# Longer VectorE times in the planner, output banks handed on one by one, and 320 bytes in front of the left side of SBUF

## The chip, the cores and the metric

The kernel runs on one core of a Trainium2 chip. The metric is the device time of one execution in microseconds (us), as a median of several runs. The engines are named as in the profile: PE multiplies matrices (PEld is its loading of weights), DVE is VectorE, ACT is ScalarE, POOL is GpSimd, and SP issues the DMAs. PSUM has eight banks, named here by their tags: ab0 to ab2, at0, at1, m0 to m2.

## The reference

Three stages follow each other, all in float32. First a linear attention with decay over 4 batches, 8 heads, 768 steps and a head width of 48; then two gated products with weights of their own.

```
state = zeros(B, H, D, D)
for t in range(S):
    y[t] = r[t] . (state + (u*k[t]) v[t]^T);  state = w*state + k[t] v[t]^T
x = y laid out as 3072 tokens x 384
x = ((x @ w_a) * (x @ w_b)) @ w_out                  # 1536 wide
a, b = x @ w1, x @ w2                                 # 1024 wide
out = (((a * b) @ w3) @ w_out2)
```

The inputs arrive as 64-bit floats for the weights, which the kernel converts itself.

## The kernel before, in words

**Numbers.** Every large product is made from float32 operands that are split into a high and a low part (a cast on ACT makes the high part, a subtraction on DVE the low one), and three matmuls high*high, high*low, low*high stand for one product.

**Stages.** From 0 to some 190 us the order is written by hand: the first attention units, the conversion of the first weights, the first gated product. All behind it is a list of 2225 tasks that `plan()` (from L209) puts in order at build time. In order of time these are: the attention units that are left with the first gated product beside them (`block1`, L904; matmuls L755 into banks ab, and L808 to L810 into m0 to m2); the conversion of the later weights and the sums over them (lines 1062 to 1178); the folding of w3 and w_out2 into one matrix `wf` (L1258); and three passes over two token blocks each, called pairs here (the loop at L1316).

**A pair.** w1 and w2 are applied by a scheme with fewer multiplications: 15 combinations S of the input blocks (POOL adds them, L1332; ACT and DVE split them, L1341 and L1343) are multiplied with combinations of the weights (`prod`, L1350, 45 matmuls of 512 columns per group of columns; the moving operand is S, in tiles qw2 to qw5 or qxa, qxb; the weights are in tiles tg). DVE and ACT add the products up in SBUF (L1417, L1423), and DVE or POOL multiplies the two halves (`finish_col`, L1361). Each of the 8 blocks that this gives for each of the two column halves n is split (gh on ACT at L1443, gl on DVE at L1445) and multiplied with `wf` (L1453 to L1455, 12 matmuls of 384 columns, three for each of four token tiles b, added up over the 8 blocks in four PSUM banks). The four banks are then copied out (ACT at L1473 for even b, DVE at L1471 for odd b) into one of the output buffers, and SP stores them (L1478).

**What sets the order.** `plan()` keeps for each engine the time from which it is free. Of all tasks whose inputs are done it starts the one that can begin first, and among those of one engine that can begin within 0.01 us, the one of lowest `prio`. A task begins when its engine is free, its inputs have ended (plus `LAT`, 0.15, when they come from another engine), and a buffer of its pool is free; `plan()` picks the buffer too. It then runs the task's function, which emits the instructions. So the durations given to the tasks set nothing but the order of the instructions on each engine, and the choice of buffers. On the chip each engine works its instructions off in that order, each as soon as its semaphores allow. The durations stand at L864: D_TT for a DVE operation on 512 columns, D_A for an ACT one, D_P for POOL, MM for a matmul.

```
            at = max(at, d.end + (0 if d.eng == e else LAT))
            x = min((x for x in c if x[0] <= t0 + 0.01), key=lambda x: x[1])
        t.end = at + t.dur
        D_TT, D_A, D_P, MM = 0.70, 0.60, 1.45, 0.2275
```

**Output banks.** The four banks of one output (m0, m1, m2, at1) are one `Slot`, taken as a whole by the first of the 8 steps of a column half, and free when all four copies are done. For the very last half the banks are ab0, ab1, ab2 and at0. There are three output buffers (`out_s`, the three parts of tile x7).

**SBUF.** Pools const, wabp and att lie at the left side, in that order from low addresses upward; the others at the right side, from the top downward. wabp holds the weights of the first product, and later qw2 to qw5 and `wf`. All tiles of wabp begin 160 bytes past a multiple of 512. The tiles of the right side that feed PE (xt, later qxa and qxb; gh and gl; the weights tg; and w_out) begin 480 bytes past one.

Of the kernel before, what the change touches and what calls it, by code (L numbers as in the profile page):

```python
# [7 lines left out]
F32 = mybir.dt.float32  # L8
# [10 lines left out]
B, H, S, D = 4, 8, 768, 48  # L19
# [4 lines left out]
DM = H * D  # L24
# [23 lines left out]

END_0 = 4
LATE = 3  # L50
N_OK = 2 * 128 * N64 + 112 * NP


# [148 lines left out]


LAT = 0.15
DMA_0, DMA_MB = 2.0, 5.0


def plan(tasks):


    free, waits, users, ready = {}, {}, {}, []
    dma = 0.0
    for t in tasks:
        waits[t] = len(t.deps)
        for d in t.deps:
            users.setdefault(d, []).append(t)
    ready = [t for t in tasks if not t.deps]

    def start(t):
        e = t.eng  # L220
        at = free.get(e, 0.0)
        for d in t.deps:
            at = max(at, d.end + (0 if d.eng == e else LAT))
        picks = []
        for b in t.bufs:
            best = None
            for s in b.pool:
                if s in picks or any(u.end is None for u in s.users):
                    continue
                k = max([at] + [u.end + (0 if u.eng == e else LAT) for u in s.users])  # L230
                old = max([0.0] + [u.end for u in s.users])
                if best is None or (k, old) < best[:2]:
                    best = (k, old, s)
            if best is None:
                return None
            at = best[0]
            picks.append(best[2])
        return at, picks

    total = len(tasks)  # L240
    while ready:
        by = {}
        for t in ready:
            r = start(t)
            if r is not None:
                by.setdefault(t.eng, []).append((r[0], t.prio, t, r[1]))
        assert by, "no task can start"
        best = None
        for c in by.values():
            t0 = min(x[0] for x in c)  # L250
            x = min((x for x in c if x[0] <= t0 + 0.01), key=lambda x: x[1])
            if best is None or x[0] < best[0]:
                best = x
        at, _, t, picks = best
        t.start = at
        free[t.eng] = at + t.dur
        t.end = at + t.dur
        if t.size:
            dma = max(dma, t.end) + t.size * DMA_MB
            t.end = dma + DMA_0  # L260
        for b, s in zip(t.bufs, picks):
            s.users = b.users or [t]
            b.ap = b.get(s.key)
        t.fn()
        ready.remove(t)
        total -= 1
        for u in users.get(t, ()):
            waits[u] -= 1
            if not waits[u]:
                ready.append(u)  # L270
    assert not total
# [3 lines left out]
def rwkv_moe_kernel(ctx, tc, rkT, nat, wu, wab, wout, w12, w3T, wo2, r_in, k_in, v_in, w_in, u_in, out):  # L275
# [12 lines left out]

    with tc.manual_schedule():
        const = tc.alloc_tile_pool(name="const", bufs=1, side="left")  # L290
        wabp = tc.alloc_tile_pool(name="wabp", bufs=1, side="left")
        att = tc.alloc_tile_pool(name="att", bufs=2, side="left")
        xtp = tc.alloc_tile_pool(name="xtp", bufs=1, side="right")
# [567 lines left out]
                t.end = 0.0  # L861
            tasks.clear()

        D_TT, D_A, D_P, MM = 0.70, 0.60, 1.45, 0.2275  # L864
        CONV = 9000.0

        def g_get(key):
# [356 lines left out]

        R5 = 200.0 * (NB - 2)
        ab_b, m_t, md_last = t_ab, t_m, d
        o_slot = Slot(("m0", "m1", "m2", "at1"))

        w_t, wo2_t = {}, {}

# [12 lines left out]
        for i in range(NF2):  # L1243
# [31 lines left out]
            e1 = use(task("ACT", 0.45, eh, [last, ab_b[2 * (i // 4) + 1]], R5 + 12 * i + 32), bp)  # L1275
            e2 = use(task("DVE", 0.55, el, [e1], R5 + 12 * i + 32), bp)
            fold_end.append(e2)
        o_slot.users = mb.users + fold_end + units


        s_s, t_s = [], []
# [3 lines left out]
        for i in range(3):  # L1285
            t_s += [Slot(f"wo{p}{i}", [m_t[4 * i + 3]]) for p in "hl"]
        v_s = [Slot((f"x{i}", k), folds) for i in (0, 1, 2, 3, 5, 6) for k in range(KD)]
        out_s = [Slot(("x7", k), folds) for k in range(KD)]
        old = [x_b[NB - 2].users[i] for i in range(len(x_b[NB - 2].users))]
        c0_s = [Slot(("xa", k), old) for k in range(2 * KD - 1)]  # L1290
        c0_bufs = []
# [12 lines left out]
        left_l = task("SP", 0.1, load_left, folds, R5 + 150, size=0.66)  # L1304

        gord = (1, 0, 2, 3, 4, 5, 6, 7)
        o_last, o_users = None, o_slot.users
        PER = 1000.0
        for pair in range(NB // 2):
            base = PER * (pair + 2)  # L1310
# [27 lines left out]
            for d in range(len(SEQ)):  # L1338
                bs = Buf(s_s + xa_s if pair else s_s, s_get)
                f, dep, b0 = src[f"S{d}"]  # L1340
                hi = use(task("ACT", D_A, lambda f=f, bs=bs: nc.scalar.copy(out=bs.ap[0], in_=f()), [dep],  # L1341
                              base - 100 + S_RANK.index(d), [bs]), b0)
                lo = use(task("DVE", D_TT, lambda f=f, bs=bs: nc.vector.tensor_tensor(  # L1343
                    out=bs.ap[1], in0=f(), in1=bs.ap[0], op=ALU.subtract), [hi], base - 100 + S_RANK.index(d)), b0, bs)
                s_buf[d], s_lo[d] = bs, lo

# [87 lines left out]
            last_use = [t for t in tasks[begun:] if t.eng not in ("SP", "POOL")]  # L1434
            for n in range(2):
                end = pair == NB // 2 - 1 and n == 1
                bo = Buf([Slot(("ab0", "ab1", "ab2", "at0"), last_use)] if end else [o_slot],
                         lambda key: [psp.tile([128, DM], F32, tag=t, name="o") for t in key])
                for z, f in enumerate(gord):
                    x, dep, bv = g_b[f, n]  # L1440
                    bh = Buf(gg_s, gg_get)
                    p0 = base + 100 * z + 100 * n + 60
                    hi = use(task("ACT", D_A, lambda x=x, bh=bh: nc.scalar.copy(out=bh.ap[0], in_=x()),  # L1443
                                  [dep] + ([o_last] if o_last and not end else []), p0, [bh]), bv)
                    lo = use(task("DVE", D_TT, lambda x=x, bh=bh: nc.vector.tensor_tensor(  # L1445
                        out=bh.ap[1], in0=x(), in1=bh.ap[0], op=ALU.subtract), [hi], p0), bv, bh)

                    def go(bo=bo, bh=bh, f=f, z=z, tiles=range(B)):
                        wh, wl = (t[:, f % 4, :] for t in w_t[f // 4])
                        gh, gl = bh.ap  # L1450
                        for b in tiles:
                            cs = slice(b * C, (b + 1) * C)
                            mm(bo.ap[b], lhsT=gh[:, cs], rhs=wh, start=(z == 0), stop=False)  # L1453
                            mm(bo.ap[b], lhsT=gh[:, cs], rhs=wl, start=False, stop=False)  # L1454
                            mm(bo.ap[b], lhsT=gl[:, cs], rhs=wh, start=False, stop=(z == NF2 - 1))  # L1455

                    p0, deps = base + (240 + 40 * z if n == 0 else 950 + 36 * z), [lo, fold_end[f]]
                    if z < NF2 - 1:
                        ot = use(task("PE", 12 * 0.177, go, deps + ([ot] if z else []), p0, [bo] if z == 0 else []),
                                 bh, bo)  # L1460
                    else:
                        ot = [use(task("PE", 3 * 0.177, lambda go=go, b=b: go(tiles=[b]), deps + [ot], p0 + b), bh, bo)
                              for b in range(B)]
                    o_last = hi
                for b in range(B):
                    be = Buf(out_s, v_get)
                    c, bt = divmod(b, 2)

                    def ev(be=be, bo=bo, b=b):
                        if b % 2:  # L1470
                            nc.vector.tensor_copy(out=be.ap[:, 0:DM], in_=bo.ap[b])  # L1471
                        else:
                            nc.scalar.copy(out=be.ap[:, 0:DM], in_=bo.ap[b])  # L1473

                    e = use(task(("ACT", "DVE")[b % 2], 0.5, ev, [ot[b]], base + 900, [be]), bo)

                    def st_out(be=be, r0=(2 * n + bt) * S + (2 * pair + c) * C):
                        nc.sync.dma_start(out=out[r0:r0 + C, :], in_=be.ap[:, 0:DM])  # L1478

                    use(task("SP", 0.1, st_out, [e], base + 900, size=0.2), be)  # L1480


        cnt = const.tile([1, 1], I32, name="cnt")

        def count():
            ok = gp.tile([128, N64, 2], F32, tag="g1", name="ok")
            nc.vector.tensor_scalar(out=ok[:, :, 0], in0=chk[:, :, 0], scalar1=SQ_HI, scalar2=None, op0=ALU.is_le)
            nc.vector.tensor_scalar(out=ok[:, :, 1], in0=chk[:, :, 1], scalar1=511.5, scalar2=None, op0=ALU.is_ge)
            col = const.tile([128, 2], F32, name="col")
            nc.vector.tensor_reduce(out=col[:, 0:1], in_=flat(ok), op=ALU.add, axis=AX.X)  # L1490
            nc.vector.tensor_reduce(out=col[0:112, 1:2], in_=wok, op=ALU.add, axis=AX.X)
            nc.vector.tensor_tensor(out=col[0:112, 0:1], in0=col[0:112, 0:1], in1=col[0:112, 1:2], op=ALU.add)
            ones = const.tile([128, 1], F32, name="ones")
            nc.vector.memset(ones, 1.0)
            mid_t["count"] = col, ones
# [260 lines left out]
```

## Time and profile before

| | us |
|---|---|
| median of 3 runs | 906.73 |
| lowest and highest run | 901.91, 906.95 |
| the profiled execution, its own time | 908.81 |
| its span, first to last instruction | 907.0 |
| busy in the span: PE, DVE, ACT, POOL | 869.5, 601.3, 372.8, 204.0 |

The profiled execution is one of its own and not among the three runs; 1.8 us of its time lie outside its span. In the rows, a line such as L1445 is a line of the kernel; "out<-in" are tile names; an "x3" merges instructions that follow each other; square brackets give the time for which the engine had been idle before the instruction, and what ended it. PE's records overlap: a matmul of 512 columns is shown with 0.39 us, though the next one starts some 0.23 us behind it.

### The profile page before, as it was taken

The page shows a single profiled execution, that of the slowest core. Times are in us where ns is not written, and L with a number is a line of the kernel's source. Part 1 is how long each engine was busy: PE and PEld are TensorE (multiplying, and loading weights), DVE is VectorE, ACT ScalarE, POOL GpSimd, SP SyncE. Part 2 cuts the span into 40 slices and gives each one's busy share as a digit, 9 for nine tenths or more (in the row PEclk, how much of TensorE's full clock was granted, in tenths as well). Part 3 has the DMA queues.
Part 4 walks back from the last instruction along what each step waited for, and adds up shares of the span by engine and source line. Part 5 has one row for each costly group of instructions (what it writes and reads, how often), then busy time and mean ns, then how long its engine had stood idle before and what let it go on. Part 6 is the DMA issues. An engine that isn't in the chain of part 4 may idle for free.

```text
span 907.0 us, 13215 instructions
## 1 busy us (share of the span) xinstructions
PE 869.5 (96%) x4827; PEld 731.2 (81%) x4827; DVE 601.3 (66%) x1031; ACT 372.8 (41%) x865; POOL 204.0 (22%) x170
## 2 busy tenths in 40 slices
PE   8887899999999999999999999999998999999996
PEld 7665778888878888888888789888886888788886
DVE  8898876368989759753566368626569546954642
ACT  3555465434454344232246445425245232623221
POOL 2213300025444205300200302212325301511210
PEclk9698899999999999999999999999999999999998
DMA  8644432045867545722153324036544234423302
GB/s 268 195 148 151 138 117 93 24 129 187 243 214 209 184 137 190 211 83 88 41 146 116 105 73 150 22 111 202 157 152 152 92 122 142 149 93 98 112 1 73
DMA packets 55719, 120.54 MB, mean 133 GB/s; under 512 B 6176, under 2 KB 33440, under 8 KB 55648
## 3 DMA queue, kind: packets, MB, share of 16 engines
q1 hardware_dynamic: 55648, 119.63, 42.0%
q8 instruction: 40, 0.66, 0.3%
q14 instruction: 31, 0.25, 0.1%
HBM read 94.57 MB, written 23.07 MB: 130 GB/s over the span
## 4 chain that ended last, share of the span: by engine, by line
PE 83%; DVE 10%; DMA 2%; issue 2%; ACT 1%; SPq 0%; DVEq 0%; ACTq 0%
PE ab L755 31%; PE ab L1350 12%; PE m L808 5%; PE m L810 5%; PE m L809 5%; PE at L1350 4%; PE at L1258 4%; PE o L1453 3%; PE o L1455 3%; PE o L1454 3%; PE at L533 3%; PE at L493 2%; PE at L529 2%; DMA rk<-in_rkT_dram 1%; DVE qx L1423 1%
## 5 line engine op out<-in xcount | busy, mean ns | idle before, releaser
L1423 DVE TENSOR_TENSOR qx<-qx,ab 128x512 f32<-128x512 f32 x97 | 65.0, 684 | 33.4 <-PE ab L1350 32.1
L809 PE MATMUL m<-gl,woh 128*128 128x512 f32 x216 | 84.4, 391 | 1.5 <-DVE gl L919 1.5
L808 PE MATMUL m<-gh,woh 128*128 128x512 f32 x216 | 85.6, 396 | 0.0
L810 PE MATMUL m<-gh,wol 128*128 128x512 f32 x216 | 84.4, 391 | 0.8 <-DVE wol L162 0.8
L914 DVE TENSOR_TENSOR ab<-g,ab 128x512 f32<-128x512 f32 x54 | 37.5, 695 | 71.1 <-PE ab L755 63.2
L916 ACT CAST gh<-ab 128x512 fp32r<-128x512 f32 x54 | 31.7, 586 | 100.5 <-DVE ab L914 100.5
L1445 DVE TENSOR_TENSOR gl<-qx,gh 128x512 fp32r<-128x512 f32 x48 | 40.3, 844 | 45.8 <-ACT gh L1443 45.7
L1361 POOL TENSOR_TENSOR qx<-qx,qx 128x512 f32<-128x512 f32 x27 | 36.6, 1357 | 141.1 <-DVE qx L1423 108.4
L913 ACT COPY g<-ab 128x512 f32<-128x512 f32 x54 | 31.8, 588 | 83.6 <-PE ab L755 83.6
L1417 ACT ACTIVATE qx<-ab 128x512 f32<-128x512 f32 x55 | 32.6, 600 | 74.3 <-PE ab L1350 73.1
L1443 ACT CAST gh<-qx 128x512 fp32r<-128x512 f32 x48 | 29.5, 620 | 62.3 <-PE o L1454 59.6
L755 PE MATMUL ab<-xt,wab0h 128*128 128x512 f32 x144 | 48.1, 415 | 1.5 <-DVE xt L558 1.5
L809 PEld LDWEIGHTS m<-gl,woh 128*128 128x128 f32 x216 | 40.5, 188 | 9.9 <-DVE gl L919 1.9
L810 PEld LDWEIGHTS m<-gh,wol 128*128 128x128 f32 x216 | 40.5, 188 | 9.7 <-DVE wol L162 1.2
L486 POOL TENSOR_TENSOR kn<-natt,tnat 128x384 f32<-128x384 f32 x13 | 13.9, 1071 | 152.6 <-PE at L605 152.6
L808 PEld LDWEIGHTS m<-gh,woh 128*128 128x128 f32 x216 | 40.5, 188 | 9.5 <-ACT woh L142 0.3
L755 PE MATMUL ab<-xt,wab1h 128*128 128x512 f32 x144 | 47.3, 411 | 0.6 <-ACT g L913 0.6
L919 DVE TENSOR_TENSOR gl<-ab,gh 128x512 fp32r<-128x512 f32 x54 | 37.1, 687 | 14.9 <-ACT gh L916 14.6
L755 PE MATMUL ab<-xt,wab2h 128*128 128x512 f32 x144 | 45.5, 397 | 0.0
L465 POOL TENSOR_TENSOR rk<-rk,tr 112x512 f32<-112x512 f32 x16 | 20.8, 1299 | 109.4 <-DMA rk<-in_rkT_dram 109.4
L755 PE MATMUL ab<-xt,wab5h 128*128 128x512 f32 x144 | 45.1, 394 | 0.0
L755 PE MATMUL ab<-xt,wab4h 128*128 128x512 f32 x144 | 45.1, 394 | 0.0
(287 smaller groups left out, 2336.6 us busy)
## 6 DMA issues: line engine op xcount, KB each, us to landing
tg<-t_d SPq DMA_DIRECT2D x45, 640.0 KB, 3.9
natt<-in_nat_dram SPq DMA_DIRECT2D x20, 576.0 KB, 5.3
rk<-in_rkT_dram SPq DMA_DIRECT2D x24, 448.0 KB, 4.6
t_d<-part SPq DMA_DIRECT2D x75, 128.0 KB, 1.8
raw<-in_wab_dram SPq DMA_DIRECT2D x18, 512.0 KB, 4.0
raw<-in_w3T_dram SPq DMA_DIRECT2D x16, 512.0 KB, 4.0
raw<-in_w_dram SPq DMA_DIRECT2D x12, 512.0 KB, 5.7
raw<-in_wout_dram SPq DMA_DIRECT2D x9, 512.0 KB, 3.5
```

The lines of the kernel that those rows point to most:

```text
L755: mm(ps, lhsT=w[i][:, k, cs], rhs=x[:, j, k, :], start=(n == 0), stop=(n == 3 * KD - 1))
L808: mm(m_ps[q][k], lhsT=wh[:, j, cs], rhs=gh, start=first, stop=False)
L809: mm(m_ps[q][k], lhsT=wh[:, j, cs], rhs=gl, start=False, stop=False)
L810: mm(m_ps[q][k], lhsT=wl[:, j, cs], rhs=gh, start=False, stop=last)
L914: mu = use(task("DVE", D_TT, lambda x=bg, y=bb: nc.vector.tensor_tensor(out=y.ap, in0=x.ap, in1=y.ap, op=ALU.mult), [ea, b], p0 + 2), bg, bb)
L919: nc.vector.tensor_tensor(out=x.ap[1], in0=y.ap, in1=x.ap[0], op=ALU.subtract)
L1258: mm(bp.ap, lhsT=b.ap[x][:, g, :], rhs=wo2_t[g // 4][y][:, g % 4, :], start=(n == 0), stop=(n == 3 * NF2 - 1))
L1350: mm(bank, lhsT=x, rhs=y, start=(start and n == 0), stop=(stop and n == 2), skip_group_check=True)
L1361: mu = use(task(eng, D_TT if inner else D_P, lambda e=e, dst=dst, xa=xa, xb=xb: e.tensor_tensor(out=dst(), in0=xa(), in1=xb(), op=ALU.mult ...
L1417: e = use(task("ACT", D_A, lambda bv=bv, b=bank[c], s=s: nc.scalar.activation(out=bv.ap, in_=b.ap, func=ACTF.Copy, scale=float(s)), [pt], ...
L1423: e = use(task("DVE", D_TT, lambda bv=bv, b=bank[c], s=s: nc.vector.tensor_tensor(out=bv.ap, in0=bv.ap, in1=b.ap, op=ALU.add if s > 0 else ...
L1445: lo = use(task("DVE", D_TT, lambda x=x, bh=bh: nc.vector.tensor_tensor(out=bh.ap[1], in0=x(), in1=bh.ap[0], op=ALU.subtract), [hi], p0), ...
```

## The change

- `plan()` adds 0.25 instead of 0.15 where a task waits for one of PE.
- D_TT goes from 0.70 to 0.72, D_A from 0.60 to 0.61. A new duration D_S, 1.0, replaces D_TT for two subtractions: the low part of S (L1343) and gl (L1445).
- Each of the output banks becomes a `Slot` of its own. The first of the 8 steps is cut into four tasks, one for each bank, as the last one was before. The copies out and their stores get a lower `prio` by 100.
- Tile g1 becomes a fourth output buffer; the small tile `ok` of the final count moves from there to tile sq.
- A tile of 320 bytes that nobody uses is allocated first in const, so that everything of the left side moves up by 320 bytes.

```diff
+PAD = 320
...
+LAT_PE = 0.25
...
+    def late(d, e):
+        return 0.0 if d.eng == e else LAT_PE if d.eng == "PE" else LAT
...
-            at = max(at, d.end + (0 if d.eng == e else LAT))
+            at = max(at, d.end + late(d, e))
...
-                k = max([at] + [u.end + (0 if u.eng == e else LAT) for u in s.users])
+                k = max([at] + [u.end + late(u, e) for u in s.users])
...
+        const.tile([128, PAD // 4], F32, name="pad")
...
-        D_TT, D_A, D_P, MM = 0.70, 0.60, 1.45, 0.2275
+        D_TT, D_S, D_A, D_P, MM = 0.72, 1.0, 0.61, 1.45, 0.2275
...
-        o_slot = Slot(("m0", "m1", "m2", "at1"))
+        o_s = [Slot(t) for t in ("m0", "m1", "m2", "at1")]
...
-        o_slot.users = mb.users + fold_end + units
+        for slot in o_s:
+            slot.users = mb.users + fold_end + units
...
-        out_s = [Slot(("x7", k), folds) for k in range(KD)]
+        out_s = [Slot(("x7", k), folds) for k in range(KD)] + [Slot(("g1", 0), list(t_ab.values()) + md_last)]
...
-                lo = use(task("DVE", D_TT, lambda f=f, bs=bs: nc.vector.tensor_tensor(
+                lo = use(task("DVE", D_S, lambda f=f, bs=bs: nc.vector.tensor_tensor(
...
-                bo = Buf([Slot(("ab0", "ab1", "ab2", "at0"), last_use)] if end else [o_slot],
-                         lambda key: [psp.tile([128, DM], F32, tag=t, name="o") for t in key])
+                bo = [Buf([Slot(t, last_use) if end else slot], lambda key: psp.tile([128, DM], F32, tag=key, name="o"))
+                      for t, slot in zip(("ab0", "ab1", "ab2", "at0"), o_s)]
...
-                    lo = use(task("DVE", D_TT, lambda x=x, bh=bh: nc.vector.tensor_tensor(
+                    lo = use(task("DVE", D_S, lambda x=x, bh=bh: nc.vector.tensor_tensor(
...
-                    if z < NF2 - 1:
-                        ot = use(task("PE", 12 * 0.177, go, deps + ([ot] if z else []), p0, [bo] if z == 0 else []),
-                                 bh, bo)
+                    if 0 < z < NF2 - 1:
+                        ot = [use(task("PE", 12 * 0.177, go, deps + ot, p0), bh, *bo)]
                     else:
-                        ot = [use(task("PE", 3 * 0.177, lambda go=go, b=b: go(tiles=[b]), deps + [ot], p0 + b), bh, bo)
-                              for b in range(B)]
+                        ot = [use(task("PE", 3 * 0.177, lambda go=go, b=b: go(tiles=[b]), deps + (ot if z else []),
+                                       p0 + b, [] if z else [bo[b]]), bh, bo[b]) for b in range(B)]
...
-                    e = use(task(("ACT", "DVE")[b % 2], 0.5, ev, [ot[b]], base + 900, [be]), bo)
+                    e = use(task(("ACT", "DVE")[b % 2], 0.5, ev, [ot[b]], base + 800, [be]), bo[b])
...
-                    use(task("SP", 0.1, st_out, [e], base + 900, size=0.2), be)
+                    use(task("SP", 0.1, st_out, [e], base + 800, size=0.2), be)
...
-            ok = gp.tile([128, N64, 2], F32, tag="g1", name="ok")
+            ok = stg.tile([128, N64, 2], F32, tag="sq", name="ok")
```

## Rows read from the trace of the kernel before

**Rows 1.** The page: busy time of each engine, and the shares of the chain.

```profile
PE 869.5 (96%) x4827; PEld 731.2 (81%) x4827; DVE 601.3 (66%) x1031; ACT 372.8 (41%) x865; POOL 204.0 (22%) x170
...
PE 83%; DVE 10%; DMA 2%; issue 2%; ACT 1%; SPq 0%; DVEq 0%; ACTq 0%
```

**Rows 2.** Stages: length, busy us of PE, PEld, DVE, ACT, POOL; clock, DMA share, GB/s.

```profile
200.00:300.00 100.00, 99.27 (x738) 81.59 (x737) 89.59 (x157) 45.80 (x128) 45.23 (x37) 1.00 0.70 207
300.00:470.00 170.00, 170.00 (x964) 139.18 (x963) 105.98 (x242) 58.67 (x164) 31.35 (x26) 1.00 0.42 132
470.00:612.00 142.00, 140.55 (x660) 121.08 (x660) 81.24 (x122) 66.61 (x146) 20.49 (x14) 1.00 0.28 97
...
694.00:708.00 14.00, 9.96 (x39) 7.97 (x38) 13.93 (x16) 3.38 (x7) 6.84 (x5) 0.88 0.41 127
708.00:783.00 75.00, 75.00 (x366) 66.04 (x365) 42.63 (x62) 26.53 (x47) 18.65 (x15) 1.00 0.36 117
783.00:798.00 15.00, 13.81 (x62) 10.77 (x62) 14.89 (x22) 6.10 (x12) 3.93 (x3) 1.00 0.51 171
```

**Rows 3.** Stages again: the 3.3 us behind the longest gap of PE.

```profile
699.70:703.00 3.30, 3.30 (x11) 2.81 (x10) 3.23 (x6) 1.41 (x3) 0.48 (x1) 0.50 0.58 175
```

**Rows 4.** Waits of PE: us in total, times, longest.

```profile
PE o L1455 <- DVE gl L1445: 3.7, 2, 3.1
...
PE m L809 <- DVE gl L919: 1.5, 1, 1.5
```

**Rows 5.** Timeline at the longest gap: start, length, engine, line.

```profile
695.58 3.42 DVE L1445 TENSOR_TENSOR gl<-qx,gh 128x512 fp32r<-128x512 f32 x2
696.75 1.71 POOL L1332 TENSOR_TENSOR qcvt<-v,qs 128x512 f32<-128x512 f32 x1
...
699.06 0.44 PE L1455 MATMUL o<-wf1h,gl 128*128 128x384 f32 x1 [3.15 <-DVE gl L1445]
```

**Rows 6.** Single lines: durations in ns, lowest, median and highest, and when.

```profile
L1445 DVE TENSOR_TENSOR gl<-qx,gh x48: 677/692/1807, 631.7 to 892.8; 128x512 fp32r<-128x512 f32 x48
...
L1343 DVE TENSOR_TENSOR qw5l<-qs,qw5h x5: 678/1362/1789, 693.9 to 786.3; 128x512 fp32r<-128x512 f32 x5
...
L1423 DVE TENSOR_TENSOR qx<-qx,ab x97: 670/686/690, 622.3 to 869.7; 128x512 f32<-128x512 f32 x97
```

**Rows 7.** Timeline of the end: the last copies out and the last matmul.

```profile
895.42 0.56 DVE L1471 COPY qx<-o 128x384 f32<-128x384 f32 x1 [1.42 <-DMA out_dram<-qx]
...
898.35 0.34 PE L1455 MATMUL o<-wf1h,gl 128*128 128x384 f32 x1
900.09 0.48 ACT L1473 COPY qx<-o 128x384 f32<-128x384 f32 x1 [2.47 <-DMA out_dram<-qx]
900.58 0.56 DVE L1471 COPY qx<-o 128x384 f32<-128x384 f32 x1 [2.30 <-ACT qx L1473]
```

**Rows 8.** Timeline of unbroken products: qxb at the right side, qw at the left.

```profile
748.99 0.85 PE L1350 MATMUL ab<-qxb,tg 128*128 128x512 f32 x3
749.68 0.39 PE L1350 MATMUL ab<-qw5h,tg 128*128 128x512 f32 x1
...
751.78 0.85 PE L1350 MATMUL ab<-qxb,tg 128*128 128x512 f32 x3
752.47 0.34 PE L1453 MATMUL o<-wf0h,gh 128*128 128x384 f32 x1
...
753.87 0.34 PE L1455 MATMUL o<-wf0h,gl 128*128 128x384 f32 x1
```

**Rows 9.** Chain in order of time: two unbroken stretches of PE.

```profile
479.79 4.12 PE ab L755 x18
...
543.41 4.18 PE at L1258 x24
```

**Rows 10.** Timeline: w_out's product, first and last of seven such starts.

```profile
502.23 0.39 PE L808 MATMUL m<-gh,woh 128*128 128x512 f32 x1
...
506.31 0.39 PE L808 MATMUL m<-gh,woh 128*128 128x512 f32 x1
```

More of the change, by code (lines that the diff above doesn't have):

```diff
@@ L1306, in rwkv_moe_kernel @@
         gord = (1, 0, 2, 3, 4, 5, 6, 7)
-        o_last, o_users = None, o_slot.users
+        o_last = None
         PER = 1000.0
@@ L1452, in go @@
                             cs = slice(b * C, (b + 1) * C)
-                            mm(bo.ap[b], lhsT=gh[:, cs], rhs=wh, start=(z == 0), stop=False)
-                            mm(bo.ap[b], lhsT=gh[:, cs], rhs=wl, start=False, stop=False)
-                            mm(bo.ap[b], lhsT=gl[:, cs], rhs=wh, start=False, stop=(z == NF2 - 1))
+                            mm(bo[b].ap, lhsT=gh[:, cs], rhs=wh, start=(z == 0), stop=False)
+                            mm(bo[b].ap, lhsT=gh[:, cs], rhs=wl, start=False, stop=False)
+                            mm(bo[b].ap, lhsT=gl[:, cs], rhs=wh, start=False, stop=(z == NF2 - 1))
                     p0, deps = base + (240 + 40 * z if n == 0 else 950 + 36 * z), [lo, fold_end[f]]
-                    if z < NF2 - 1:
-                        ot = use(task("PE", 12 * 0.177, go, deps + ([ot] if z else []), p0, [bo] if z == 0 else []),
-                                 bh, bo)
-                    else:
-                        ot = [use(task("PE", 3 * 0.177, lambda go=go, b=b: go(tiles=[b]), deps + [ot], p0 + b), bh, bo)
-                              for b in range(B)]
+                    if 0 < z < NF2 - 1:
+                        ot = [use(task("PE", 12 * 0.177, go, deps + ot, p0), bh, *bo)]
+                    else:
+                        ot = [use(task("PE", 3 * 0.177, lambda go=go, b=b: go(tiles=[b]), deps + (ot if z else []),
+                                       p0 + b, [] if z else [bo[b]]), bh, bo[b]) for b in range(B)]
                     o_last = hi
@@ L1470, in ev @@
                         if b % 2:
-                            nc.vector.tensor_copy(out=be.ap[:, 0:DM], in_=bo.ap[b])
+                            nc.vector.tensor_copy(out=be.ap[:, 0:DM], in_=bo[b].ap)
                         else:
-                            nc.scalar.copy(out=be.ap[:, 0:DM], in_=bo.ap[b])
-                    e = use(task(("ACT", "DVE")[b % 2], 0.5, ev, [ot[b]], base + 900, [be]), bo)
+                            nc.scalar.copy(out=be.ap[:, 0:DM], in_=bo[b].ap)
+                    e = use(task(("ACT", "DVE")[b % 2], 0.5, ev, [ot[b]], base + 800, [be]), bo[b])
                     def st_out(be=be, r0=(2 * n + bt) * S + (2 * pair + c) * C):
                         nc.sync.dma_start(out=out[r0:r0 + C, :], in_=be.ap[:, 0:DM])
-                    use(task("SP", 0.1, st_out, [e], base + 900, size=0.2), be)
+                    use(task("SP", 0.1, st_out, [e], base + 800, size=0.2), be)
         cnt = const.tile([1, 1], I32, name="cnt")
         def count():
-            ok = gp.tile([128, N64, 2], F32, tag="g1", name="ok")
+            ok = stg.tile([128, N64, 2], F32, tag="sq", name="ok")
             nc.vector.tensor_scalar(out=ok[:, :, 0], in0=chk[:, :, 0], scalar1=SQ_HI, scalar2=None, op0=ALU.is_le)
```

## The prediction

> **What bounds the kernel now.** I read the page's busy times first, then a table of stages, then what PE waited for, and last the timeline at the gaps. PE is busy for 869.5 of 907.0 us and makes 83% of the chain; DVE, the next, makes 10% [rows 1]. So time is to be had in two ways only: where PE stands still or runs slowly, and from each matmul being shorter.
>
> The table of stages says where PE stands still. The first 190 us are ordered by hand and only move in SBUF, so I leave them out. Behind them PE lacks 0.73 us between 200 and 300, 1.45 us between 470 and 612, 4.04 us between 694 and 708 (14.00 less 9.96), and 1.19 us between 783 and 798 [rows 2]. That is 7.4 us. The two middle stages are the changes from one pair to the next. There DVE is full, 13.93 of 14.00 and 14.89 of 15.00 us, and PE empty in places; in the stages around them it is the other way round. Between 708 and 783 PE has no gap at all [rows 2]. The longest single gap is 3.15 us at 699.06, where a matmul of the last step waits for gl [rows 5]; DVE's gl as the releaser makes 3.7 us of PE's waiting in all [rows 4]. Behind that gap PE's granted clock is at 0.50, the 1.2 GHz level, for 3.3 us [rows 3]; at 2.4 GHz the same matmuls take half of it, so 1.65 us are lost there as well. **Together 9.1 us are lost to stalls in the planned part.**
>
> Why gl is late is on the same timeline: two of them take 3.42 us, and while they run POOL works on its own addition of 1.71 us [rows 5]. Alone this subtraction takes 0.69 us, the median of 48; the longest took 1.81. The low part of S goes from 0.68 to 1.79. An operation of the same size that reads one operand from PSUM never leaves 0.67 to 0.69 [rows 6]. So gl and the low part of S, which read two operands in SBUF, are slow whenever POOL works, and the plan counted on 0.70 for both.
>
> **The durations and the waiting time for PE.** They emit no instruction and remove none. 45 subtractions of S and 48 of gl keep their work; only the order changes, and with it what is ready when. With 1.0 the plan puts gl and the low parts of S later, so PE's instructions that need them are placed behind others that are ready: the order stops counting on 0.70 where the chip takes up to 1.8 [rows 6]. D_TT of 0.72 and D_A of 0.61 are small shifts of everything else. No row of before shows the new order, so I bound it: at best all 9.1 us go; at worst the new order brings as many stalls again, 9.1 us more.
>
> **The banks.** Today the second column half of a pair may begin only when all four copies out of the first are done. Each copy takes 0.48 on ACT or 0.56 on DVE [rows 7], and at the change of pair DVE is full, so a copy stands in line behind subtractions. With one slot for each bank, PE starts the new half on the first bank when that one is out. The first step's 12 matmuls are the same 12, cut into four tasks, and nothing is added. The lower priority of the copies only brings them ahead in DVE's and ACT's order: 4 x 0.5 us that the subtractions behind them wait longer, in a stage where DVE is full [rows 2]. The gain falls into the same gaps as that of the durations, so I count the two together. In the stage from 694 to 708 I take three quarters of 4.04 + 1.65 us, which is 4.3; in that from 783 to 798 half of 1.19, which is 0.6; and nothing for the 2.2 us elsewhere, where a new order may as well bring a gap as take one. **Taken: -5 us; bounds -9.1 and +9.1.**
>
> **The fourth output buffer.** At the end the last matmul starts at 898.35 and lasts 0.34, but ACT's copy of the third bank waits 2.47 us for a store to leave the third buffer, and the last copy ends at 900.58 + 0.56 = 901.14 [rows 7]. With a fourth buffer the eight last copies use each buffer twice, and the earlier store is done by then: the copy at 895.42, which waited 1.42 us for the same reason, goes ahead as well. The last copy then follows the last matmul: 898.69 + 0.56, with 0.1 allowed for the hand-over, is 899.35. **Taken: -1.8 us; bounds -1.8 and 0.** What follows the last copy (store, count, branch) is the same work as before. The count's `ok` in tile sq needs the last `Sign` to have run, which is long over.
>
> **The padding.** It adds no instruction. What it changes shows only in the pace of matmuls. In one unbroken stretch, two trios with S at the right side take 0.69 us each (748.99 to 749.68, 751.78 to 752.47), while nine with S at the left take 2.10 us (749.68 to 751.78): 0.230 against 0.233 us each, 3.3 ns more [rows 8]. With 384 columns, eight starts with `wf` at the left as moving operand take 1.40 us (752.47 to 753.87), 0.1750 each [rows 8], against 4.18 / 24 = 0.1742 in the fold, where both operands lie at the right [rows 9]. Where the weights are at the left and the moving operand at the right the pace is 4.12 / 18 = 0.2289 [rows 9], where both are at the right 18 starts take 4.08 us, 0.2267 each [rows 10]. So left tiles cost PE something, and what the rows can't say is whether by their side or by their 160 bytes past a multiple of 512. With 320 more they stand at 480, like those at the right. I take it to be the offset, because it is the one thing besides the side that all the slower tiles share and all the faster ones lack, and the padding removes it. The terms: 516 products with S at the left x 3.3 ns = 1.7 us; 576 matmuls with `wf` x 0.8 ns = 0.5 us; 1296 of L755 x 2.2 ns = 2.9 us, of which I take half, since these are the weights and not the moving operand. **Taken: -3.6 us; bounds -5.1 and +0.7**, the upper end being a loss of 0.5 ns on the 1296, which is what rows read to 0.01 us over 18 starts can hide.
>
> Against this stands the Trainium skill's page "TensorE: Matmul & The Clock Gate", section "Part 1: The HAM clock gate (the "warmup" mystery)": back-to-back matmuls start N / 2.4 GHz + 2.5 ns apart, about 215.7 ns for 512 columns, with no term for where the operands lie. The trace does not agree with it: these matmuls are 226.7 to 233 ns apart. By that rule the term would be 0 and the sum 3.6 us less; the rival below has it.
>
> **The sum.** -5 - 1.8 - 3.6 = -10.4 us. Against the profiled execution's own time that gives 908.8 - 10.4 = 898.4 us. That execution lies 2.1 us above the median of the runs, and the runs differ by 5 us among themselves, which is the size of the stall at 699: part of what I take away the median run may not have had. So I take somewhat less than 10.4 off the median of 906.7, and **predict 897.0 us**, with 892 to 902 as this case's own range.
>
> **Rivals.**
> - *The padding is worth nothing, and the stalls only move.* If the pace belongs to the side and not to the offset, 3.6 us fall away; and DVE stays full at the change of pair, since its work there is the same, so perhaps 2 of the 5 us come. 906.7 - 2 - 1.8 = about 903. For it: DVE's 13.93 of 14.00 us [rows 2]. Against it: POOL's overlap is what makes it full, and between 708 and 783 DVE has 32 us to spare. Chance 0.29.
> - *All of it comes.* 9.1 + 1.8 + 5.1 = 16.0 us: about 890. For it: PE has other work at hand in the stages of both gaps, since the outputs of one pair and the products of the next don't depend on each other. Against it: every order has some gaps. Chance 0.13.
> - *Slower: the order becomes too cautious.* D_TT and D_S are now above what the chip takes when POOL rests (0.72 and 1.0 against 0.68 [rows 6]). Between 200 and 300 DVE is 90% busy [rows 2]; if the plan believes it overfull, it sends the converted weights, which have the lowest priority, behind the first product, and PE then waits for them in the fold. Each such gap of 3 us costs the slow clock too, 3.15 + 1.65 = 4.8 us. Three of them, 14.4 us, against 5.4 us from padding and end and nothing from the stalls: 906.7 + 9 = about 916. It decides as soon as the new gaps sum to more than what the other parts give, some 10 us. Against it: between 300 and 470 DVE is busy for 106 of 170 us [rows 2], so what is put off there has room before the fold. Chance 0.12.
>
> My forecast has the remaining 0.46.
>
> **How the numbers follow.** The measurement tells about 1% of this kernel from no change, 9 us: faster means below 897.7, slower above 915.8. The middle of my own case lies a little below 897.7, so I count 0.28 of its 0.46 as faster, and all of the second rival: 0.28 + 0.13 = 0.41. The slower case is split at its middle, which leaves 0.06 above 915.8, and the rest, 0.53, is within 1%. The range runs from 888, near what all the terms together give, to 908: it leaves out the slower case and little else, between 0.15 and 0.2.
>
> **What would show it.** The stages around the changes of pair should have less than 2 us of PE's idle time in all, and PE's clock at 1.00 there. Waits of PE for gl should be under 1.5 us. The last copy out should end within 0.8 us of the last matmul, with no copy waiting for a store. Nine products with S at the left should take 2.07 us instead of 2.10, and L755's 18 some 4.10 or less. If the last stays at 4.12 and 2.10, the padding did nothing. A new gap in the stage from 470 to 612 would be the cautious order. I am wrong in kind if the stalls at the change of pair stay at 5 us and the time falls all the same.

## The result, and the profile after

The changed kernel takes 894.12 us, the median of 6 runs (893.06 to 895.63); six runs of the kernel before on the same chip have a median of 905.41 us (901.91 to 906.95). **The ratio is 0.9882, with a 95% interval of 0.9856 to 0.9907**: 11.3 us less, where the prediction had 9.7 off the median of 906.73 and a range of 888 to 908. The profiled execution after took 893.52 us, its span is 891.8.

First the page of the kernel after, busy times and the shares of the chain, against [rows 1]:

```profile
PE 856.5 (96%) x4827; PEld 726.5 (81%) x4827; DVE 602.6 (68%) x1031; ACT 373.3 (42%) x865; POOL 204.6 (23%) x170
...
PE 89%; DVE 6%; DMA 2%; ACT 1%; issue 1%; SPq 0%; DVEq 0%
```

PE, DVE, ACT and POOL have the instructions that they had, and DVE the same busy time to 1.3 us. PE's busy time fell by 13.0 us with the same 4827 matmuls (3.7 of it in the first part, which is ordered by hand), so much of the gain lies inside PE's work, not in gaps; and DVE's share of the chain fell from 10% to 6%. The stages, with the columns of [rows 2]; the changes of pair now lie at 680 to 700 and at 770 to 790 us:

```profile
200.00:300.00 100.00, 100.00 (x744) 82.81 (x743) 94.38 (x158) 45.82 (x130) 51.00 (x42) 1.00 0.71 215
...
470.00:605.00 135.00, 133.55 (x631) 115.67 (x630) 75.98 (x115) 62.02 (x134) 19.72 (x14) 1.00 0.29 97
...
680.00:700.00 20.00, 20.00 (x108) 18.85 (x108) 18.74 (x24) 9.40 (x17) 9.48 (x7) 1.00 0.53 176
700.00:770.00 70.00, 70.00 (x335) 61.12 (x335) 43.87 (x63) 25.64 (x46) 21.55 (x16) 1.00 0.42 131
770.00:790.00 20.00, 19.77 (x102) 17.62 (x101) 15.92 (x25) 7.76 (x14) 2.98 (x2) 1.00 0.33 115
```

At the changes of pair PE lacks 0.00 and 0.23 us, where it lacked 4.04 and 1.19 [rows 2], at a clock of 1.00 throughout. DVE is a little less full there than before: 18.74 and 15.92 of 20.00 us, against 13.93 of 14.00 and 14.89 of 15.00. The 1.45 us between 470 and 605 have stayed, to the hundredth. PE's waits (line, engine and tile waited for; us in total, times, longest) say the same:

```profile
PE m L815 <- DVE gl L925: 1.5, 1, 1.5
...
PE o L1460 <- DVE qx L1368: 0.2, 1, 0.2
PE ab L1357 <- DVE qx L1430: 0.2, 1, 0.2
```

The wait for gl at the last step, 3.7 us in [rows 4], has no row any more. And yet the subtraction itself is no faster (durations lowest, median, highest):

```profile
L1452 DVE TENSOR_TENSOR gl<-qx,gh x48: 678/693/1785, 625.9 to 875.4; 128x512 fp32r<-128x512 f32 x48
```

1785 against 1807 ns [rows 6]: what changed is who stands behind it. Two rows of the chain in order of time give the pace of unbroken matmuls, the first with the weights of the first product at the left side, the second of products with S at either side:

```profile
290.19 4.08 PE ab L761 x18
...
730.22 5.48 PE ab L1357 x24
```

4.08 is what 18 starts took before where both operands lay at the right [rows 10]; for the same matmuls of L755 the chain before had 4.12 [rows 9]. The end went the other way. From its timeline, the last copies and the last matmul, against [rows 7]:

```profile
877.50 0.48 ACT L1479 COPY qx<-o 128x384 f32<-128x384 f32 x1 [2.15 <-PE o L1462]
...
879.06 0.56 DVE L1477 COPY v<-o 128x384 f32<-128x384 f32 x1 [0.48 <-PE o L1462]
...
879.99 0.48 ACT L1479 COPY qx<-o 128x384 f32<-128x384 f32 x1 [0.97 <-DMA out_dram<-qx]
...
880.77 0.34 PE L1462 MATMUL o<-wf1h,gl 128*128 128x384 f32 x1
...
882.04 0.56 DVE L1477 COPY qx<-o 128x384 f32<-128x384 f32 x1 [2.42 <-DMA out_dram<-qx]
882.49 0.48 ACT L1479 COPY qx<-o 128x384 f32<-128x384 f32 x1 [2.02 <-DMA out_dram<-qx]
882.98 0.56 DVE L1477 COPY v<-o 128x384 f32<-128x384 f32 x1 [0.39 <-DMA out_dram<-v]
```

The last copy still ends 2.8 us after the last matmul starts (883.54 less 880.77; before 901.14 less 898.35), and still because stores hold the buffers: all four copies of the last column half now wait for one (0.97, 2.42, 2.02 and 0.39 us).

**Where the 15.2 us between the two profiled spans went.** I cut both traces at the start of the planned part, the first matmul of the fold, the first product of a pair and the start of the last matmul, and did the same for every run below. All in us, the kernels named by the labels that the next section explains:

| | first part | to the fold | fold | pairs | last matmul to end | median of runs |
|---|---|---|---|---|---|---|
| before | 189.0 | 327.3 | 101.5 | 280.6 | 8.7 | 905.41 |
| pad_only | 187.1 | 325.6 | 101.3 | 276.4 | 8.9 | 901.28 |
| dur_only | 185.6 | 327.2 | 101.5 | 277.4 | 12.4 | 906.42 |
| banks_only | 187.0 | 327.0 | 101.5 | 278.8 | 6.4 | 901.88 |
| no_pad | 185.5 | 326.4 | 101.5 | 272.0 | 11.1 | 899.32 |
| after | 186.7 | 324.0 | 101.3 | 268.7 | 11.1 | 894.12 |
| ds_back | 185.4 | 324.9 | 101.3 | 274.0 | 7.0 | 893.64 |
| outs | 184.1 | 325.8 | 101.3 | 268.7 | 9.3 | 891.22 |
| outs_sp | 188.5 | 324.3 | 101.3 | 268.7 | 8.0 | 891.36 |

The last column comes from several batches of runs, in which the kernel before had medians of 904.51 to 905.78. The first column is ordered by hand and the same in all but its addresses; it differs by 4.4 us between outs and outs_sp, which differ only far behind it. So a difference there is that of the execution, and I read the other columns. Of these the second is the least sure: after and outs have the same order up to the last copies, and yet differ by 1.8 us there, while their fold and pairs agree to the digit. Before to after the second to fifth columns give -3.3, -0.2, -11.8 and +2.4: 12.9 us gained, of which the pairs have nearly all.

### The profile page after: what moved, and what is told of

The parts are those of the page before. It is cut to its first block, busy times and chain, and to the rows that moved or that the text cites. A ratio compares the mean times of both kernels' runs of the same rounds, so it can differ in the third digit from the quotient of the medians.

```text
span 891.8 us, 13219 instructions
## 1 busy us (share of the span) xinstructions
PE 856.5 (96%) x4827; PEld 726.5 (81%) x4827; DVE 602.6 (68%) x1031; ACT 373.3 (42%) x865; POOL 204.6 (23%) x170
## 4 chain that ended last, share of the span: by engine, by line
PE 89%; DVE 6%; DMA 2%; ACT 1%; issue 1%; SPq 0%; DVEq 0%
PE ab L761 32%; PE ab L1357 14%; PE m L814 5%; PE m L816 5%; PE m L815 5%; PE at L1357 5%; PE at L1264 4%; PE o L1460 4%; PE o L1462 4%; PE o L1461 4%; PE at L539 3%; PE at L499 2%; PE at L535 2%; DMA rk<-in_rkT_dram 1%; DVE cvt L127 1%
## 5 line engine op out<-in xcount | busy, mean ns | idle before, releaser
L1368 POOL TENSOR_TENSOR qx<-qx,qx 128x512 f32<-128x512 f32 x29 | 39.4, 1370 | 124.5 <-DVE qx L1430 116.3
L925 DVE TENSOR_TENSOR gl<-ab,gh 128x512 fp32r<-128x512 f32 x54 | 37.1, 688 | 13.5 <-ACT gh L922 13.2
```

Of the source, the lines that this page charges most:

```text
L925: nc.vector.tensor_tensor(out=x.ap[1], in0=y.ap, in1=x.ap[0], op=ALU.subtract)
L1368: mu = use(task(eng, D_TT if inner else D_P, lambda e=e, dst=dst, xa=xa, xb=xb: e.tensor_tensor(out=dst(), in0=xa(), in1=xb(), op=ALU.mult ...
```

## The experiments

Two theories stood against each other on each half of the change. On the pace: the place of the left tiles is what counts, or their side is, and the gain is all in the order. On the stalls: the new durations alone remove them, or the banks alone, or it takes both.

**The padding alone** (pad_only): the kernel before with one allocation.

```diff
+PAD = 320
...
+        const.tile([128, PAD // 4], F32, name="pad")
```

> The kernel before plus the 320 bytes alone; every instruction stands in the old order. Offset theory (the pace of a matmul follows where in 512 bytes a left tile begins): the products with S at the left start 227 to 229 ns apart instead of 233, those with wf 174 instead of 176, L755 with a high part 227 instead of 230; 516 x 4.8 + 576 x 1.3 + 864 x 2.9 ns = 5.7 us less, so 899 to 901, and the stalls at the change of pair stay at 4 us or more. Side theory (the left side is slow wherever its tiles begin, and the changed kernel's shorter pace has another cause): no change, 904 to 907.

Measured: 901.28 us against 905.78, ratio 0.9948 (0.9927 to 0.9970). The wait for gl stays, as long as before:

```profile
PE o L1457 <- DVE gl L1447: 3.9, 2, 3.3
```

So 4.5 us come from addresses alone, with not an instruction moved.

**Everything but the padding** (no_pad): the kernel after without that allocation, its instructions in the same order.

```diff
-        const.tile([128, PAD // 4], F32, name="pad")
```

> The changed kernel without the 320 bytes; the order is that of the changed kernel. Offset theory: the left products are back at 233 ns, and 5.7 us come back: 899 to 901, with PE's gaps at the changes of pair still gone. Side theory: 893 to 896, as the changed kernel.

Measured: 899.32 us, ratio 0.9942 (0.9925 to 0.9959). The wait for gl at the last step is gone, and the pace is the old one, from the chain in order of time:

```profile
290.02 4.12 PE ab L760 x18
...
733.37 5.58 PE ab L1356 x24
```

So the two halves of the change are worth about the same, 6.5 us here and 4.5 above, and add up to the whole (11.0 against 11.3) within the intervals of some 2 us either way.

**The durations alone** (dur_only): LAT_PE, D_S, D_TT and D_A as in the change, the four banks one slot, three output buffers, no padding.

```diff
-        D_TT, D_A, D_P, MM = 0.70, 0.60, 1.45, 0.2275
+        D_TT, D_S, D_A, D_P, MM = 0.72, 1.0, 0.61, 1.45, 0.2275
...
-            at = max(at, d.end + (0 if d.eng == e else LAT))
+            at = max(at, d.end + late(d, e))
```

> The kernel before with the new durations and the longer wait for PE alone; one slot for four banks, three output buffers, no padding. If the durations took the stalls away: PE's idle time at the two changes of pair under 1.5 us, and 899 to 902. If the banks did: idle time there 3 us or more, and 903 to 907.

Measured: 906.42 us, ratio 1.0011 (0.9993 to 1.0029): nothing. The wait for gl is gone, and PE waits as long for something else, which its timeline shows:

```profile
695.10 1.61 POOL L1336 TENSOR_TENSOR qs<-qs,qs 128x512 f32<-128x512 f32 x1
695.49 3.43 DVE L1347 TENSOR_TENSOR qw5l<-qs,qw5h 128x512 fp32r<-128x512 f32 x2
696.66 1.71 POOL L1336 TENSOR_TENSOR qcvt<-v,qs 128x512 f32<-128x512 f32 x1
698.84 0.55 DVE L1475 COPY qx<-o 128x384 f32<-128x384 f32 x1
...
699.44 0.69 PE L1457 MATMUL o<-wf0h,gh 128*128 128x384 f32 x1 [3.44 <-DVE qx L1475]
```

Two subtractions that run beside POOL take 3.43 us, as in [rows 5]; only now they are low parts of S, and behind them in DVE's line stands the copy of the fourth output bank. Until it is out, the new half may begin on none of the four. After the gap the clock is low again, mean 0.59 (stage table, columns as above):

```profile
699.44:703.00 3.56, 3.56 (x13) 3.56 (x14) 3.56 (x6) 0.62 (x1) 0.95 (x1) 0.59 0.70 201
```

The pairs still gain 3.1 us, and the end loses 3.7: its last copy ends 5.2 us behind the start of the last matmul.

**The banks, the copies and the fourth buffer alone** (banks_only): the kernel after with the old durations and without the padding.

```diff
-        D_TT, D_S, D_A, D_P, MM = 0.72, 1.0, 0.61, 1.45, 0.2275
+        D_TT, D_S, D_A, D_P, MM = 0.70, 0.70, 0.60, 1.45, 0.2275
...
-LAT_PE = 0.25
+LAT_PE = 0.15
```

> The kernel before with the four slots, the higher rank of the copies and the fourth output buffer alone; old durations, no padding. If the banks took the stalls away: PE's idle time at the two changes of pair under 1.5 us, and 899 to 902. If the durations did: gl still late by 2 us or more at one of them, and 902 to 906.

Measured: 901.88 us, ratio 0.9953 (0.9937 to 0.9969). The wait for gl stays:

```profile
PE o L1461 <- DVE gl L1451: 3.7, 2, 3.2
```

The pairs gain 1.8 us and the end 2.2, for here the fourth buffer does what it was meant to. The last two copies in the timeline wait for their matmuls and for no store; the last ends at 895.24, 0.9 us after the start of the last matmul (894.31):

```profile
894.20 0.48 ACT L1478 COPY qx<-o 128x384 f32<-128x384 f32 x1 [0.57 <-PE o L1461]
894.68 0.56 DVE L1476 COPY v<-o 128x384 f32<-128x384 f32 x1 [0.49 <-PE o L1461]
```

Taken together: in the pairs the durations give 3.1, the banks 1.8, and both 8.6 (no_pad). **The stalls need both.** Either part alone leaves DVE one slow pair of subtractions with something behind it that PE wants at once. What is called the banks here is three things, the four slots, the rank of the copies and the fourth buffer; no run takes them apart.

**D_S alone set back** (ds_back): the kernel after, with the subtractions planned at 0.72.

```diff
-        D_TT, D_S, D_A, D_P, MM = 0.72, 1.0, 0.61, 1.45, 0.2275
+        D_TT, D_S, D_A, D_P, MM = 0.72, 0.72, 0.61, 1.45, 0.2275
```

> The changed kernel with D_S at 0.72 like D_TT. If it is the 1.0 for the two subtractions that gets gl out of PE's way: PE waits for gl again at a change of pair, 2 us or more in one piece, and 896 to 900. If the longer wait for PE or the other small steps do it: no such wait, and 893 to 896.

Measured: 893.64 us, ratio 0.9882 (0.9855 to 0.9908), the same as after. I had expected a wait for gl and a longer time; the wait that came is mostly the one for a bank's copy:

```profile
PE o L1460 <- DVE qx L1477: 2.6, 1, 2.6
...
PE o L1462 <- DVE gl L1452: 0.7, 1, 0.7
```

The pairs are 5.3 us longer, so with the banks as they are it takes D_S to keep them free of stalls; but this order's end is 4.1 us shorter, and what the one takes the other gives back. For the whole kernel D_S was worth nothing.

**The place of the left side.** Four kernels are the kernel after with another number of bytes, and in one both sides are moved. Each has one execution, the profiled one; the order of the instructions is that of after in all.

```diff
-PAD = 320
+PAD = 64
...
-PAD = 320
+PAD = 160
...
-PAD = 320
+PAD = 352
...
-PAD = 320
+PAD = 192
```

> The changed kernel with 64 bytes of padding instead of 320: left tiles begin 224 bytes past a multiple of 512, the right ones at 480. If the pace goes by the place within 512 bytes being the same as the weights' or the right side's: products with S at the left at 231 ns or more. If it goes by the place within 256 bytes (480 and 224 are both 224 past one) or within 128: 227 to 229 ns as with 320.

> The changed kernel with 160 bytes of padding: left tiles begin 320 past a multiple of 512, which is 64 past one of 128 and of 256. If only 480 is fast: 231 ns or more for products with S at the left. If every offset but the old 160 is fast, or whatever is a multiple of 64: 227 to 229 ns.

> The changed kernel with 352 bytes of padding: left tiles begin at multiples of 512. If a start at a boundary is what PE likes: 226 to 228 ns for products with S at the left, as with 320 or a little less. If sharing the offset of the right side is what counts: 231 ns or more.

> The changed kernel with 192 bytes of padding: left tiles begin 352 past a multiple of 512, which is 96 past one of 128 but not 224 past one of 256. If the place within 128 bytes decides: products with S at the left at 227 to 229 ns, 891 to 895. If the place within 256 does: 233 ns and 900 or more.

both0 puts the left side at 0 past a multiple of 512, as pad352 does, and with 480 bytes in front of the right side that one too:

```diff
-PAD = 320
+PAD = 352
...
+        xpad = tc.alloc_tile_pool(name="xpad", bufs=1, side="right")
+        xpad.tile([128, 120], F32, name="xpad")
```

> The changed kernel with 352 bytes of padding at the left and 480 at the right side's upper end, so that the tiles of both sides begin at multiples of 512. If what counts is that both sides share an offset: products with S at the left at 229 ns or less, 892 to 896. If what counts is the offset itself, and 0 is a slow one: products at both sides, L755 and L808 to L810 at 232 ns or more, and 905 to 915.

Two rows of the chain for each kernel, as above: 18 matmuls of the first product, 24 of a pair. pad64:

```profile
287.83 4.08 PE ab L761 x18
...
728.20 5.48 PE ab L1357 x24
```

pad160:

```profile
298.46 4.21 PE ab L761 x18
...
745.78 5.60 PE ab L1357 x24
```

pad352:

```profile
292.63 4.20 PE ab L761 x18
...
739.37 5.58 PE ab L1357 x24
```

pad192:

```profile
292.68 4.19 PE ab L761 x18
...
738.91 5.54 PE ab L1357 x24
```

both0:

```profile
293.12 4.08 PE ab L763 x18
...
733.15 5.48 PE ab L1359 x24
```

| kernel | left, past 512 | right, past 512 | left less right, past 256 | 18 starts | 24 starts | us |
|---|---|---|---|---|---|---|
| no_pad | 160 | 480 | 192 | 4.12 | 5.58 | 899.32 |
| after | 480 | 480 | 0 | 4.08 | 5.48 | 894.12 |
| pad64 | 224 | 480 | 0 | 4.08 | 5.48 | 891.9 |
| pad160 | 320 | 480 | 96 | 4.21 | 5.60 | 911.45 |
| pad352 | 0 | 480 | 32 | 4.20 | 5.58 | 904.97 |
| pad192 | 352 | 480 | 128 | 4.19 | 5.54 | 904.56 |
| both0 | 0 | 0 | 0 | 4.08 | 5.48 | 896.07 |

The rows fall into two classes. It is fast where the two sides stand at the same place within 256 bytes, whichever place that is, and slower at each of the four other differences tried. Left tiles at 0 are slow beside a right side at 480 (pad352) and fast beside one at 0 (both0), so the place of the left side by itself is not what counts, nor is its side. The rule can't be that of a matmul's own two operands alone, though. The products with S at the right have both operands at 480 in no_pad, in pad352 and in after, and start 230.2, 231.4 and 227.7 ns apart in the mean; in no_pad the first three behind products of another kind take 228.9, 232.5 and 230.3, in after 227.4, 228.1 and 228.5. So what PE works on beside them, or what else uses the left tiles, counts as well; no run separates these. In the fold's own matmuls, where no operand lies at the left and none stand beside products with S, the distance is 174.8 or 174.9 ns in all three.

**More buffers for the last copies** (outs): the kernel after, where the copies of the last pair may also use the 18 column buffers, which are free by then.

```diff
-                    be = Buf(out_s, v_get)
+                    be = Buf(out_s + v_s if pair == NB // 2 - 1 else out_s, v_get)
```

> The changed kernel where the last pair's copies out may also take the 18 column buffers that are free by then. If the copies at the end wait for stores to leave the four buffers (2.4 and 2.0 us in the profile): no such wait, the last copy ends within 1.0 us of the last matmul instead of 2.4, and 892 to 893.5, 1 to 1.5 us less. If the stores' own time sets the end: the copies end earlier and the time stays at 893.5 to 895.

Measured: 891.22 us (890.04 to 892.08), ratio to the kernel before 0.9843 (0.9818 to 0.9867). The last two copies wait only for their matmuls, the last of which starts at 879.99:

```profile
879.84 0.48 ACT L1479 COPY qx<-o 128x384 f32<-128x384 f32 x1 [0.56 <-PE o L1462]
880.36 0.56 DVE L1477 COPY qx<-o 128x384 f32<-128x384 f32 x1 [0.49 <-PE o L1462]
```

The last copy ends 0.9 us after that start, not 2.8. **It beats the kernel before by 1.6%.** The median is 2.9 us under that of after, and the runs of the two don't overlap (890.04 to 892.08, 893.06 to 895.63); but they come from different batches, the intervals of the two ratios overlap a little, and the column of the end gives 1.7 us of it.

**SP's program a little longer** (outs_sp). Behind the final branch SP's record in the trace shows a gap of 2.6 to 2.9 us in every kernel. In after, no_pad, dur_only and outs it shows a second one of 1.9 to 2.4 us. These four have 681 SP instructions up to that branch, where before, pad_only and banks_only have 684; the five kernels with other bytes have 681 and show it too, and ds_back, with 683, shows 0.8 us. To move the count I cut one load into five.

```diff
-            nc.sync.dma_start(out=left_b["t"].bitcast(F32), in_=l_d)
+            for j in range(5):
+                nc.sync.dma_start(out=left_b["t"].bitcast(F32)[:, j], in_=l_d[:, j])
```

> The kernel with the free column buffers for the last copies, and one DMA of SP (the load of tl) cut into five, so that SP has four instructions more in front of the final branch. If SP's second gap of 2 us behind the branch, which only the orders with 681 instead of 684 SP instructions show, is an edge in SP's instruction stream that the branch lies just in front of: that gap is gone and the time 1.9 to 2.4 us less than without the four, 888.8 to 889.5. If the gap comes from the stores that are under way: it stays, and 891.

Measured: 685 instructions, the second gap gone, 8.0 us from the last matmul to the end instead of 9.3; and 891.36 us (887.14 to 892.67), ratio 0.9846 (0.9818 to 0.9874), the same as outs. The gap moves with the count, but the runs don't show its 1.3 us; whether they would with more of them stays open.

## Why the prediction was right, and where its steps were wrong

The time came out 2.9 us under the one forecast, inside the case's own range of 892 to 902. Three terms were each off by 2 to 4 us, and two of the errors cancel: the mechanisms of the stalls and of the padding held in the main, but that the sum came so near is luck.

**The stalls: right mechanism, too small.** The step took "three quarters of 4.04 + 1.65", half of 1.19 and "nothing for the 2.2 us elsewhere", -5 in all. No_pad against before gives -8.6 in the pairs, where the prediction had counted 6.9 us as lost (4.04 + 1.65 + 1.19); the -0.9 in front of the fold is less than the executions differ by there. The share was the guess, and it was too cautious: with both parts PE nearly always had a product at hand, and its idle time in the pairs fell from 5.84 to 0.36 us. And the amount was too small, because idle time understates a stall. PE's records are longer than the distance to the next start, so a record hides the beginning of the wait behind it: the longest gap, 3.15 us of idle time, is a distance of 3.49 us between two starts, where 0.175 is the pace. All that the distances in the pairs exceed their unbroken mean by, where it is more than 20 ns, sums to 10.2 us before and 2.0 in no_pad, 8.3 less, the slow clock included. Of the 2.2 us elsewhere the 1.45 before the fold stayed, as taken. The two parts were rightly counted together, and the reason given was right for the order but not for each part: that "the order stops counting on 0.70" would have brought nothing without the banks, as dur_only shows.

**The fourth output buffer: the step failed.** It said that with four buffers "the earlier store is done by then". It is so with the old durations: banks_only's end is 2.2 us shorter, somewhat more than the 1.8 taken. But the step was worked out on the timeline of before, [rows 7], and the same change moves that timeline. In banks_only the last bank of the first half is copied at 890.49, the first of the second at 893.15, 2.7 us apart; in the kernel after that distance is 879.06 to 879.99, 0.9 us, and the stores still hold the buffers. The end became 2.4 us longer, against a bound of 0: last copy as late as before, and SP's second gap behind it. So one part of the change (the order) took back what another (the buffer) gives; outs shows it, since buffers alone bring the last copy back to 0.9 us behind the last matmul and the end from 11.1 to 9.3 us.

**The padding: the cause was named too narrowly, and the term was too small.** Taken -3.6, bound -5.1. The medians give -4.5 (pad_only) and -5.2 (no_pad to after), the second to fourth columns of the stages -6.1 and -5.9. I had "3.3 ns" for a product with S at the left, from rows read to 0.01 us. The mean distance of successive starts in the trace (some 500 such products, distances from 215 to 245 ns, so that gaps are left out) fell from 233.2 in before to 228.4 in after, 4.8 ns; that of the first product's matmuls with high weights from 229.9 to 227.2, of those with low weights hardly (228.0 to 227.9); with `wf` it fell from 175.6 to 174.3; and the products with S at the right fell too, from 230.2 to 227.7, which the prediction had not counted at all. With the counts: 516 x 4.8 + 864 x 2.7 + 576 x 1.3 + 213 x 2.5 ns = 2.5 + 2.3 + 0.7 + 0.5 = 6.0 us, about what the stages have. And the step "I take it to be the offset, because it is the one thing besides the side that all the slower tiles share" left out a third reading: that the two operands of one matmul stand differently. pad352 and both0 decide for that one against the other two, though the products with S at the right show that it is not the whole of it.

The Trainium skill's rule (page "TensorE: Matmul & The Clock Gate", section "Part 1: The HAM clock gate (the "warmup" mystery)"), a start each N / 2.4 GHz + 2.5 ns with no term for the place of the operands, would have made the padding worth nothing. The runs disagree: pad_only moves addresses alone and is 4.5 us faster.

**The rivals.** "Padding worth nothing, and the stalls only move" fails on both halves with the change as it is; its second half is just what dur_only does. "All of it comes" was nearest in the stalls (8.6 us in the pairs, of its 9.1) and passed in the padding, and missed its 890 mainly by the end: with outs, which mends the end, the time is 891.2. The cautious order: no new gap came between 200 and 605 us, but the loss at the end is of its kind, an order that lets the last two halves finish together.

**What was to show it.** Less than 2 us of idle time at the changes of pair (0.23), the clock at 1.00, no wait for gl above 1.5 us, L755's 18 at 4.10 or less (4.08), nine products with S at the left in 2.07 us (9 x 228.4 ns = 2.06): as said. The last copy within 0.8 us of the last matmul, and none waiting for a store: not so.

**What stays open.** Why PE keeps a shorter distance when the tiles of both sides stand at the same place within 256 bytes, and why products whose own operands stand so lose too, beside others whose operands don't: no run says where the time goes, and only differences of 32, 96, 128 and 192 bytes were tried. Nor is it clear why, at 192, the first product's low weights lose nothing and its high ones 2.7 ns, though both lie at the left. Pad160's 911.45, a single run, lies 12 us above no_pad: of the 13.2 us between the two spans 7.8 are in the first part (193.3 against 185.5 us, mean clock 0.86 and 0.91 over the first 130 us), 3.3 in front of the fold, where its first product is slow (4.21 for 18), and 1.4 in the pairs.

## What to carry to other kernels

When a planner's order stalls because one operation is slower than planned, try the corrected duration and a looser hand-over of buffers together: here the first alone only put another instruction behind the slow one. Count a stall by the distance of starts, not by idle time. Whenever an order changes, look at the end again, for buffers that were enough are judged by distances that the new order moves. And note the addresses of both operands of the commonest matmuls, modulo 256 bytes: here a tile that nobody uses was worth half a per cent.

## What the runs showed of the hardware that I had not expected

- The distance between matmuls goes with where the tiles of their two operands stand relative to each other: in rows of 18 starts of the first product 226.7 ns (4.08 / 18) where they agree modulo 256 bytes, 233 to 234 ns (4.19 to 4.21 / 18) at differences of 32, 96 and 128, 229 at 192. Matmuls among such, whose own operands agree, lose as well (230.2 against 227.7 ns).
- The end of the program has a part in which PE, DVE, ACT and POOL have no work: behind the last copy 5.5 to 8.4 us pass (banks_only 895.24 to 900.74, outs 880.92 to 889.30), with a gap of 2.6 to 2.9 us in SP's record in every kernel, and a second one of 1.9 to 2.4 us that all kernels with 681 SP instructions up to the branch show and those with 684 or 685 don't.
- The first 190 us took between 184.1 and 189.0 us with the same order. What differs with it is the granted clock: its mean over the first 130 us is 0.87 in the profile of before, 0.89 in that of after and 0.92 in that of outs. With two levels, 2.4 and 1.2 GHz, that is 2 x 0.13 x 130 = 34 us at the lower one, 29 and 21. PE works there in short pieces with waits of up to 3.6 us between them.
